# Moving transposes of exponentials behind the transposes of x, and two row sums into the following stage, in a fused attention and MLP kernel

## The chip, the cores and the metric

One core of a Trainium2 chip. The metric is the device time of one execution in microseconds; the median of three runs of the kernel before is 269.20 us (269.05 to 269.24).

The names of the engines are those of the profile: PE multiplies matrices (PEld is its loading of weights), DVE is the vector engine, ACT the scalar engine, POOL the general one, and SP issues transfers. Each has its own program and they meet at semaphores.

## The reference

Linear attention (a softmax of q over the head's 64 columns, one of k over the 576 positions) over 8 batches with 8 heads, followed by a layer norm and an MLP with a residual:

```python
q_s = exp(q - max(q, -1));  q_s = q_s / sum(q_s, -1)
k_s = exp(k - max(k, 2));   k_s = k_s / sum(k_s, 2)
kv  = einsum('bhsd,bhse->bhde', k_s, v)
x   = einsum('bhsd,bhde->bhse', q_s, kv)       # then to (8, 576, 512)
xn  = (x - mean(x)) / sqrt(var(x) + 1e-6) * g_ln
out = x + relu(xn @ w_ch1) @ w_ch2             # 512 -> 2048 -> 512
```

## The kernel before

**Chunks and stages.** The positions of each batch are cut into 512 main ones (4 tiles of 128) and 64 remaining ones. The 8 batches' main parts are chunks 0 to 7; the remaining 8 x 64 rows together are a ninth, `C9`, the last chunk. The kernel has one stage for each chunk: PE does the two MLP multiplications of chunk c, while the attention of chunk c+1 and the first steps of c+2 are worked in between. I call "stage c" the stage that multiplies chunk c.

**An order written out by hand.** In each stage `mlp_steps(c)` gives a list of PE steps with a weight each, and a list `side` gives (position, function) pairs for all other work. `run` walks through the PE steps, adds up the weights, and emits a side function as soon as the sum has reached its position. The order in which they are emitted is the order of the instructions on each engine: each engine's program is fixed, and nothing is sorted anew later. A position is thus a place in a queue, not a time.

**The two multiplications.** From stage 2 on both are done with seven products in place of eight (a Strassen form). The first, `mm1_fast`, takes positions 0 to 56: two halves, each with two groups (0 and 1, then 2 and 3) of seven products of four matmuls, in the order 1, 5, 6, 2, 7, 3, 4; each product is done for both groups of the half, and a matmul of 256 columns weighs 0.5. So product 5 takes positions 4 to 8, product 6 takes 8 to 12, product 7 takes 16 to 20, product 4 takes 24 to 28. All products go to banks of PSUM, six in rotation (`mm_ps`), by names x, b, c. Products 1, 6, 7 and 4 of a group accumulate into its bank x. Between them, DVE reads the bank: `add_5` (L775) after product 6, `out_22` (L778) after product 7. Each is emitted right after the last matmul of its group, and the group's next product into that bank waits for it:

```python
plan = (
    (1, "x", True, seed), (5, "b", True, copy_5), (6, "x", False, add_5),
    (2, "c", False, lambda g: out_relu(g, "c", 0, 0)), (7, "x", False, out_22),
    (3, "b", False, lambda g: out_relu(g, "b", 0, 1)),
    (4, "x", False, lambda g: out_relu(g, "x", 1, 0)),
)
```

The second, `mm2_fast`, takes positions 56 to 112, 8 for each product in the order 1, 5, 6, 2, 7, 3, 4. At its end DVE scales the results, adds x and writes the output tiles (`y_quarter`, L610, from the banks named c, e, b, a), after two additions (`add_u`, L627). The next stage's product 5 takes the banks that these steps free.

**Side work of a stage c.** For chunk c+1 (`attn_fast`): the reciprocal of the row sums of exp(q) (`recip_q`, L859); `kv_all`, 40 small matmuls and on DVE L342 and L344; per tile t the attention product `po_mm` and, on DVE, `x_fast` (L421 and L407, which write x and the scaled xn). Two transfers transpose xn, `xn_T`, two tiles each, from SP's queue; then `sum_x` (L248) forms four differences of the transposed x, which products 5, 6, 7 and 4 of the next stage take. They run on POOL, for chunk 7 the second on DVE, for the last chunk all on DVE. For chunk c+2 (`prep_fast`): exp(q) on ACT (`exp_q`), its transpose by a transfer of SP (`eq_T`, L256), its row sums on DVE in two halves (`reduce_q`, L210, 128x1024 to 128x16), exp(k) (`exp_k`). SP's queue also holds the loads of the next batch (`load_batch`), emitted at position 1, and in stage 6 those of the last chunk (`load_qrem`).

Batch 3 and the last chunk are apart: batch 3's exponentials, transpose and first sum stand in `second_side` (stage 1) and its second sum at position 8 of stage 2; the last chunk's exponentials, transpose and both sums stand in stage 6 (at the end of the file), and what follows of it in `attn_rest` (stage 7).

Of the kernel before, what the change touches and what calls it, by code (L numbers as in the profile page):

```python
# [20 lines left out]
def kernel(  # L21
# [31 lines left out]
    C9 = B  # L53
# [795 lines left out]

    def prep_fast(b):  # L850

        s = [(57, lambda: exp_q(b, 0, 4)), (65, lambda: exp_q(b, 2, 4)), (70, lambda: eq_T(b))]
        s += [(81, lambda: reduce_q(b, 0, 2)), (91, lambda: reduce_q(b, 2, 2))]
        s += [(81, lambda: exp_k(b, 0, 4)), (98, lambda: exp_k(b, 2, 4))]
        s += [(106, lambda: prep_kvrem(b))]
        return s

    def recip_q(c):
        nc.vector.reciprocal(eqs[c][2], eqs[c][1])  # L859

    def attn_fast(c):

        s = [(8, lambda: reduce_q(3, 2, 2))] if c == 3 else []
        s += [(22 if c == 3 else 2, lambda: recip_q(c))]
        s += [(12, lambda: kv_all(c))]
        s += [(40, lambda: start_x(c))]
        for t, (p0, p1) in enumerate(((48, 53), (57, 59), (65, 67), (73, 75))):
            s += spread([lambda t=t, i=i: po_mm(c, t, i) for i in range(NP)], p0, p1)
            s += [(p1, lambda t=t: x_fast(c, t)), ((66, 74, 87, 91)[t], lambda t=t: square_sum(c, t))]
        s += [(61, lambda: xn_T(c, 0, 2)), (78, lambda: xn_T(c, 2, 2)), (95, lambda: rstd_op(c))]  # L870
        s += [((84, 100 if c == C9 - 1 else 88, 92, 101)[i], lambda i=i: sum_x(c, i)) for i in range(4)]
        return s

    def second_side():

        s = [(p, lambda i=i: quarter_w2(i, 1)) for i, p in enumerate((8.5, 13, 44, 46))]
        s += [(8.0, lambda: xn_pT(1, 3, nc.vector))]
        s += [(3, lambda: exp_q(2, 0, 4)), (7, lambda: exp_q(2, 2, 4)), (7.2, lambda: eq_T(2))]
        s += [(42, lambda: square_sum(1, 2)), (67, lambda: square_sum(1, 3)), (71, lambda: rstd_op(1))]
        s += [(7.3, lambda: load_batch(3, (2,), eqTs[2][0:1, T - 1, NP - 1, 0:4])), (31, lambda: load_batch(3, (0,)))]  # L880
        s += [(9 + 2 * j, lambda j=j: cast_v(2, j)) for j in range(2)]
        s += [(7.4, lambda: load_v(3))]
        s += [(93 + j, lambda j=j: cast_v(3, j)) for j in range(2)]
        s += [(15 + 3 * t, lambda t=t: reduce_q(2, t, 2)) for t in (0, 2)]
        s += [(36, lambda: recip_q(2))]
        s += [(18, lambda: exp_k(2, 0, 4)), (22, lambda: exp_k(2, 2, 4)), (26, lambda: prep_kvrem(2))]
        s += [(41, lambda: kv_all(2))]
        s += [(46, lambda: start_x(2))]
        for t, (p0, p1) in enumerate(((52, 54), (57, 59), (62, 65), (70, 74))):
            s += spread([lambda t=t, i=i: po_mm(2, t, i) for i in range(NP)], p0, p1)  # L890
            s += [(p1, lambda t=t: x_fast(2, t)), ((73, 82, 88, 94)[t], lambda t=t: square_sum(2, t))]
        s += [(60, lambda: xn_T(2, 0, 2)), (77, lambda: xn_T(2, 2, 2)), (100, lambda: rstd_op(2))]
        s += [(75, lambda: exp_q(3, 0, 4)), (79, lambda: exp_q(3, 2, 4)), (85, lambda: eq_T(3))]
        s += [(97, lambda: reduce_q(3, 0, 2))]
        s += [(97, lambda: exp_k(3, 0, 4)), (108, lambda: exp_k(3, 2, 4)), (113, lambda: prep_kvrem(3))]
        s += [(p, lambda i=i: sum_w1(i, 1)) for i, p in enumerate((30, 47, 58, 64))]
        s += spread([lambda i=i: sum_x(2, i) for i in range(4)], 95, 108)
        return s

    def attn_rest():  # L900

        s = [(2, lambda: recip_q(C9)), (4, lambda: start_x(C9))]
        for t, (p0, p1, p2) in enumerate(((14, 22, 46), (44, 54, 62), (58, 66, 69), (67, 75, 77))):
            s += [(p0, lambda t=t: [po_mm(C9, t, i) for i in range(NP)])]
            s += [(p1, lambda t=t: x_fast(C9, t)), (p2, lambda t=t: square_sum(C9, t))]
        s += [(61, lambda: xn_T(C9, 0, 2)), (78, lambda: xn_T(C9, 2, 2)), (88, lambda: rstd_op(C9))]
        return s + spread([lambda i=i: sum_x(C9, i) for i in range(4)], 102, 104)
# [179 lines left out]
    with tc.manual_schedule(  # L1087
        engines={mybir.EngineType.PE, mybir.EngineType.DVE, mybir.EngineType.Activation,
                 mybir.EngineType.SP, mybir.EngineType.Pool}
    ):  # L1090
        first_batch()
        load_behind(1, (2, 0))
        load_w2(2)
        load_behind(1, (1,))
        load_w2(3)
        load_behind(2)

        def po_x(c, t):
            for i in range(NP):
                po_mm(c, t, i)  # L1100
            x_fast(c, t)

        run(
            mlp_steps(0),
            [
                (0.5, lambda: xn_pT(0, 1, nc.scalar)),
                (2.5, lambda: (q0_rest(2), x_fast(0, 2))),
                (3.2, lambda: eq_pT(0, 3, nc.scalar)),
                (7, lambda: (q0_rest(3), x_fast(0, 3))),
                (11, lambda: xn_pT(0, 2, nc.scalar)),  # L1110
                (15, lambda: xn_pT(0, 3, nc.scalar)),
                (20, g_columns),
                (24, lambda: square_sum(0, 2)),
                (28, lambda: square_sum(0, 3)),
                (34, lambda: (x_copy(0, 0), square_po(0, 1))),
                (36, lambda: x_copy(0, 1)),
                (37, lambda: nc.vector.tensor_scalar_mul(out=xs[0][3][:, 0, 1:2], in0=xs[0][3][:, 0, 1:2], scalar1=float(DM))),
                (38, lambda: rstd_op(0)),
            ]
            + [(62, lambda: exp_q(1, 0, 4)), (64, lambda: exp_q(1, 2, 4))]  # L1120
            + [(67 + t, lambda t=t: reduce_q(1, t)) for t in range(T)]
            + [((74, 78, 86, 90)[t], lambda t=t: eq_pT(1, t, nc.scalar)) for t in range(T)]
            + [(78, lambda: nc.vector.reciprocal(eqs[1][2], eqs[1][1]))]
            + [(80, lambda: exp_k(1, 0, 4)), (84, lambda: exp_k(1, 2, 4))]
            + [(26 + 4 * i, lambda i=i: scale_w1(i % KO1, i // KO1)) for i in range(2 * KO1)]
            + [(p, lambda i=i: quarter_w2(i, 0)) for i, p in enumerate((55, 58, 60, 62))]
            + [(98.5 + 0.4 * j, lambda j=j: cast_v(1, j)) for j in range(2)]
            + [(p, lambda i=i: sum_w1(i, 0)) for i, p in enumerate((80, 84, 88, 92))]
            + [(100.4, lambda: prep_kvrem(1))]
            + [(100.5, lambda: kv_mm(1, range(T))), (102.0, lambda: (kv_mm(1, range(T, T + 1)), kv_out(1), start_x(1)))]  # L1130
            + [(108.0, lambda: po_x(1, 0)), (110.0, lambda: po_x(1, 1))]
            + [(113.0, lambda: po_x(1, 2)), (114.9, lambda: xn_pT(1, 0, nc.scalar)), (115.9, lambda: square_sum(1, 0))]
            + [(115.9, lambda: po_x(1, 3)), (121.0, lambda: xn_pT(1, 1, nc.scalar)), (122.0, lambda: square_sum(1, 1))]
            + [(128.0, lambda: xn_pT(1, 2, nc.scalar))]

        )
        for c in range(1, B):
            side = []
            if c == 1:
                side += second_side()  # L1140
            else:
                if c + 1 < B:
                    side += attn_fast(c + 1)
                else:
                    side += attn_rest()
                if c + 2 < B:
                    side += [(1, lambda b=c + 2: load_batch(b))]
                    side += [(26, lambda b=c + 2: load_v(b))]
                    side += prep_fast(c + 2)
            if c == B - 2:  # L1150
                side += [(1, load_qrem)]
                side += spread([lambda r=r: exp_qrem(r) for r in range(T)], 58, 80)
                side += [(84, lambda: eq_T(C9))]
                side += [(84 + 4 * t, lambda t=t: reduce_q(C9, t, 2)) for t in (0, 2)]
            sums = [(57, 0)] if c == FAST else [(p, i) for i, p in enumerate((30, 41) if c == B - 1 else (30, 33, 41))]
            run(mlp_steps(c), side + [(at, lambda i=i: sum_h(0, i)) for at, i in sums])
        run(mlp_steps(C9), [(33 + 3 * i, lambda i=i: sum_h(0, i)) for i in range(2)])
# [30 lines left out]
```

## Time and profile before

| what | value |
|---|---|
| median of 3 runs | 269.20 us |
| the profiled execution | 269.13 us |
| its span, first to last instruction | 267.3 us |
| granted clock of PE, mean | 0.993 |
| PE busy | 259.4 us, 97% |
| DVE busy | 219.9 us, 82% |
| ACT busy | 178.9 us, 67% |
| POOL busy | 90.8 us, 34% |
| row sums `reduce_q` on DVE | 20 of 1.05 us mean, 20.6 us |
| transposes of exp(q) issued by SP | 7, landing after 4.9 us (median) |
| transposes of xn issued by SP | 14, landing after 3.5 us (median) |

The profile gives for each instruction its engine, the line of the kernel, the tiles that it writes and reads (out<-in) and its start and duration. In the timeline, neighbours of one line and form are merged (x2, x8), with the idle time of the engine before them and what ended it in brackets. On DVE an instruction starts up to 0.09 us before the one ahead of it is reported as ended, so costs in a full queue are spacings from start to start rather than durations. A matmul of 256 columns is listed with 0.27 us, but the next one starts 0.109 us after it.

### The profile page before, as it was taken

What the parts mean: (1) busy time and instruction counts of PE and PEld (TensorE: products, weight loads), DVE (VectorE), ACT (ScalarE), POOL (GpSimd) and SP (SyncE); (2) the same over time, 40 slices, a digit from 0 to 9 for tenths busy, and PEclk for the clock granted to TensorE, in tenths of its full rate; (3) what the DMA queues carried; (4) which work ended last, traced back from release to release, by engine and by line L of the source; (5) the groups of instructions that cost most, each with busy time, mean ns of one, the idle gap of its engine ahead of it and who ended that gap; (6) DMA issues with size and microseconds to landing.
All of it is one profiled execution on the core that took longest, in us unless ns stands there. A gap on an engine that the chain in (4) does not pass through costs nothing. (4 is left out here: it accounts for less than half of the span.)

```text
span 267.3 us, 6695 instructions
## 1 busy us (share of the span) xinstructions
PE 259.4 (97%) x2631; PEld 219.1 (82%) x2634; DVE 219.9 (82%) x471; ACT 178.9 (67%) x349; POOL 90.8 (34%) x145
## 2 busy tenths in 40 slices
PE   8899999999999999999999999999999899999993
PEld 6688855675888998899889988998898788888882
DVE  7864885887999899789978997898799968877872
ACT  4667881697966886688668866886678378438400
POOL 6943126213059203940394059206400800030000
PEclk9899999999999999999999999999999999999999
DMA  6999999978975996799699939995805430422014
GB/s 209 222 201 207 323 225 297 268 189 263 180 142 161 324 163 94 240 288 97 117 264 265 142 71 274 267 154 108 256 2 97 100 122 4 78 81 78 2 39 118
DMA packets 82329, 45.00 MB, mean 168 GB/s; under 512 B 58037, under 2 KB 78521, under 8 KB 82298
## 3 DMA queue, kind: packets, MB, share of 16 engines
q0 software_dynamic: 32800, 22.29, 46.1%
q1 hardware_dynamic: 48906, 21.77, 36.5%
q10 hardware_dynamic: 592, 0.52, 0.6%
q8 instruction: 20, 0.33, 0.5%
q14 instruction: 11, 0.09, 0.1%
HBM read 36.70 MB, written 9.44 MB: 173 GB/s over the span
## 5 line engine op out<-in xcount | busy, mean ns | idle before, releaser
L599 PEld LDWEIGHTS <-hs 128*128 128x128 bf16 x512 | 49.5, 98 | 5.7
L744 PEld LDWEIGHTS <-w_q 128*128 128x128 bf16 x448 | 42.9, 98 | 6.7 <-DVE ot L610 1.0
L248 POOL TENSOR_TENSOR tq<-xnT 128x256 bf16<-128x256 bf16 x24 | 15.6, 665 | 78.1 <-DMA xnT<-xn 40.2
L599 PEld LDWEIGHTS <-hT 128*128 128x128 bf16 x384 | 37.2, 98 | 4.4
L744 PEld LDWEIGHTS <-w1g 128*128 128x128 bf16 x336 | 32.2, 98 | 3.9
L599 PE MATMUL ba<-w_q,hs 128*128 128x256 bf16 x256 | 31.7, 273 | 0.0
L775 DVE TENSOR_TENSOR bb<-bx,s 128x512 f32<-128x512 f32 x28 | 18.2, 695 | 13.9 <-ACT s L772 13.9
L744 PE MATMUL bx<-tq,w_q 128*128 128x256 bf16 x224 | 29.0, 273 | 0.0
L768 ACT COPY bc<-bx 128x512 f32<-128x512 f32 x28 | 15.2, 596 | 16.8 <-PE bx L744 16.8
L421 DVE SCALAR_TENSOR_TENSOR x<-po,rq 128x512 bf16<-128x512 f32 x34 | 23.3, 686 | 2.4 <-PE po L370 2.1
L395 ACT ACTIVATE scrap<-x,mv 128x512 bf16<-128x512 bf16 x32 | 23.0, 719 | 1.6 <-DVE x L421 1.3
L616 POOL DMA_DIRECT2D out_dram<-ot x28 | 15.4, 557 | 24.1 <-DVE ot L610 24.0
L786 ACT ACTIVATE hT<-bc 128x512 bf16<-128x512 f32 x28 | 15.3, 595 | 12.1 <-PE bc L744 12.1
L583 DVE TENSOR_TENSOR hs<-hT 128x1024 bf16<-128x1024 bf16 x32 | 21.7, 686 | 1.3 <-ACT hT L786 1.2
L210 DVE TENSOR_REDUCE zq<-eq 128x16 f32<-128x1024 bf16 (+1 forms) x20 | 20.6, 1047 | 0.9 <-ACT eq L193 0.8
L370 PE MATMUL po<-kv_sb,eqT 128*128 128x128 bf16 x128 | 21.1, 219 | 0.0
L786 ACT ACTIVATE hT<-bb 128x512 bf16<-128x512 f32 x28 | 15.2, 595 | 8.8 <-PE bb L744 8.8
L778 DVE TENSOR_TENSOR hT<-bx,s 128x512 bf16<-128x512 f32 x28 | 18.0, 685 | 3.2 <-PE bx L744 3.2
L624 ACT COPY s<-ba 128x512 f32<-128x512 f32 x15 | 8.7, 578 | 12.5 <-PE ba L599 7.8
L599 PE MATMUL ba<-w_sb,hT 128*128 128x256 bf16 x128 | 16.7, 273 | 0.0
L599 PE MATMUL bb<-w_q,hs 128*128 128x256 bf16 x128 | 16.6, 273 | 0.0
L772 ACT COPY s<-bb 128x512 f32<-128x512 f32 x28 | 15.7, 624 | 1.0 <-PE bb L744 0.9
(152 smaller groups left out, 555.3 us busy)
## 6 DMA issues: line engine op xcount, KB each, us to landing
out_dram<-ot POOLq DMA_DIRECT2D x32, 256.0 KB, 6.1
qt<-in_q_dram SPq DMA_DIRECT2D x5, 1024.0 KB, 5.9
kt<-in_k_dram SPq DMA_DIRECT2D x5, 1024.0 KB, 12.8
w_sb<-in_moe_w_ch_dram POOLq DMA_DIRECT2D x4, 512.0 KB, 17.2
qt<-in_q_dram POOLq DMA_DIRECT2D x2, 1024.0 KB, 15.0
kt<-in_k_dram POOLq DMA_DIRECT2D x2, 1024.0 KB, 15.7
vm<-in_v_dram POOLq DMA_DIRECT2D x16, 128.0 KB, 11.2
w_raw<-in_moe_w_ch_dram POOLq DMA_DIRECT2D x3, 512.0 KB, 12.6
```

Of the source, the lines that this page charges most:

```text
L210: nc.vector.reduce_sum(eqs[c][1][:, ts], eqs[c][0][:, ts], axis=AX.X)
L248: eng.tensor_tensor(out=dst[:, t], in0=x[:, t], in1=y[:, t], op=ALU.subtract)
L370: nc.tensor.matmul(pobox["p"][:, i * P : i * P + P], eqTs[c][:, t, i, :], kv_sb[:, c, i, :], start=True, stop=True,)
L395: nc.scalar.activation(scrap, x[:, t], AF.Square, bias=mv[:, t, 0:1], scale=-float(DM), accum_out=mv[:, t, 1:2],)
L421: nc.vector.scalar_tensor_tensor(x[:, t].rearrange("p (h d) -> p h d", h=H), in0=pobox[c, t].rearrange("p (h d) -> p h d", h=H), scalar=1. ...
L583: nc.vector.tensor_tensor(out=dst, in0=x, in1=y, op=op)
L599: nc.tensor.matmul(hbox[bank][:, t], lhsT, rhs, start=first and (own or t == 0) and k == 0, stop=k == KH - 1, skip_group_check=True)
L744: nc.tensor.matmul(dst[:, q], lhsT, rhs, start=first and q == 0 and ko == 0, stop=ko == 1, skip_group_check=True)
L772: nc.scalar.copy(at[g, "s"], at[g, "b"])
L775: nc.vector.tensor_tensor(out=at[g, "b"], in0=at[g, "x"], in1=at[g, "s"], op=ALU.add)
L778: nc.vector.tensor_tensor(out=h_out(g, 1, 1), in0=at[g, "x"], in1=at[g, "s"], op=ALU.add)
L786: nc.scalar.activation(h_out(g, odd, half), at[g, name], AF.Relu)
```

## The change

Three sorts of moves; no operation is added or removed.

1. The transpose of exp(q) of batches 4 to 7 (`prep_fast`, stages 2 to 5) goes from position 70 to 79. The second transpose of xn is at 78, the first at 61, so the three now follow one another as xn, xn, exp(q) on SP.
2. Batch 3's first row sum leaves the end of stage 1 (position 97) for position 10 of stage 2, the second goes there from 8 to 18, the reciprocal from 22 to 26.
3. The last chunk's second row sum leaves the end of stage 6 (position 92) for position 6 of stage 7, where the reciprocal goes from 2 to 12; its transpose and first sum go from 84 to 88 in stage 6.

```diff
 def prep_fast(b):
-        s = [(57, lambda: exp_q(b, 0, 4)), (65, lambda: exp_q(b, 2, 4)), (70, lambda: eq_T(b))]
+        s = [(57, lambda: exp_q(b, 0, 4)), (65, lambda: exp_q(b, 2, 4)), (79, lambda: eq_T(b))]
...
 def attn_fast(c):
-        s = [(8, lambda: reduce_q(3, 2, 2))] if c == 3 else []
-        s += [(22 if c == 3 else 2, lambda: recip_q(c))]
+        s = [(p, lambda t=t: reduce_q(3, t, 2)) for t, p in ((0, 10), (2, 18))] if c == 3 else []
+        s += [(26 if c == 3 else 2, lambda: recip_q(c))]
...
 def second_side():
-        s += [(97, lambda: reduce_q(3, 0, 2))]
...
 def attn_rest():
-        s = [(2, lambda: recip_q(C9)), (4, lambda: start_x(C9))]
+        s = [(6, lambda: reduce_q(C9, 2, 2)), (12, lambda: recip_q(C9)), (4, lambda: start_x(C9))]
...
             if c == B - 2:
-                side += [(84, lambda: eq_T(C9))]
-                side += [(84 + 4 * t, lambda t=t: reduce_q(C9, t, 2)) for t in (0, 2)]
+                side += [(88, lambda: eq_T(C9))]
+                side += [(88, lambda: reduce_q(C9, 0, 2))]
```

## The prediction, before the changed kernel had run

> **What bounds the kernel now.** I began with the page: how much of the span PE (TensorE) is busy. Then a stretch of one stage.
>
> ```profile
> span 267.3 us, 6695 instructions
> PE 259.4 (97%) x2631; PEld 219.1 (82%) x2634; DVE 219.9 (82%) x471; ACT 178.9 (67%) x349; POOL 90.8 (34%) x145
> ```
>
> ```profile
> 122.20:148.40 26.20, 26.20 (x283) 23.42 (x281) 22.82 (x49) 19.61 (x39) 12.05 (x18) 1.00 1.05 186
> ```
>
> In the second row the columns after the stretch are its length and the busy time of PE, PEld, DVE, ACT, POOL. PE is busy for all of 26.20 us, so the stages of batches 3 to 6 cannot get shorter by removing waits. The first products of the stages of batches 2 to 7 and of the last chunk start at 79.50, 106.06, 132.27, 158.48, 184.69, 210.90 and 238.36 us: the stages of 3 to 6 take 26.21 each, that of 2 takes 26.56 and that of 7 27.46. What PE still waits for there is in its list of waits (total, times, longest):
>
> ```profile
> PE bb L744 <- DVE ot L610: 0.9, 2, 0.7
> PE bb L744 <- DVE kt L1079: 0.2, 1, 0.2
> ```
>
> Matmuls of 256 columns start 0.109 us apart. Counted from start to start, the first row is two holes in stage 7: 212.63 instead of 211.77 (0.86) and 213.41 instead of 213.07 (0.34). The second is one hole in stage 2: 81.16 instead of 80.82 (0.34; I use 0.33). All three are bank "b" of product 5 waiting until DVE has read the last stage's results out of that bank (L610).
>
> **The vector engine at these places.** The timeline (start, duration) across the start of stage 2:
>
> ```profile
> 76.16 1.21 DVE L210 TENSOR_REDUCE zq<-eq 128x16 f32<-128x1024 bf16 x1
> ...
> 81.04 1.21 DVE L210 TENSOR_REDUCE zq<-eq 128x16 f32<-128x1024 bf16 x1
> ...
> 82.29 1.30 DVE L775 TENSOR_TENSOR bb<-bx,s 128x512 f32<-128x512 f32 x2
> ```
>
> The first sum (76.16) stands ahead of the six result steps L610; the second behind them, in the slot before the addition L775, which waits for product 6 anyway. And in stage 6, which has no sums there:
>
> ```profile
> 187.13 1.30 DVE L775 TENSOR_TENSOR bb<-bx,s 128x512 f32<-128x512 f32 x2 [1.10 <-ACT s L772]
> ...
> 188.34 0.17 DVE L342 RECIPROCAL rzk<-pkv 128x4 f32<-128x4 f32 x1
> 188.54 0.86 DVE L344 TENSOR_TENSOR kv_sb<-pkv,rzk 64x256 bf16<-64x256 f32 x2
> ...
> 189.69 1.29 DVE L778 TENSOR_TENSOR hT<-bx,s 128x512 bf16<-128x512 f32 x2 [0.28 <-PE bx L744]
> ...
> 190.80 1.04 PE L744 MATMUL bx<-tq,w1g 128*128 128x256 bf16 x8
> ```
>
> The 8 matmuls at 190.80 are product 4 of groups 0 and 1; each overwrites the bank "x" that output step L778 of its group reads. L778 of group 1 starts 190.29 and ends 190.98; product 4 of group 1 starts at 190.80 + 4 x 0.109 = 191.24. So there is 0.26 us of slack in that place, and a sum takes 1.2.
>
> **The change, part by part.**
>
> *Batch 3's sums.* The first leaves the end of stage 1. Its neighbours there run without gaps, so it holds them for 76.16 to 77.29, 1.13 us. Once gone, the last L610 pair waits for the end of product 4 instead, as at the start of stage 6, where PE has no hole: gain 0.33, all of it.
>
> Both sums then stand at positions 10 and 18 of stage 2. Four matmuls weigh 2, so in program order position 10 falls between L775 of group 0 and of group 1, and 18 between L778 of group 0 and of group 1. The slot ahead of L775, where one was free, stays empty. I put them into stage 6's rows: L775 of group 0 at 187.13; +0.61 to the next start; +1.13 sum; +0.60 L775 of group 1; +0.20 L342; +0.78 the two L344; +0.61 L778 of group 0; +1.13 sum; +0.69 L778 of group 1 until its end: 192.88. With 0.05 to PE's start (212.58 to 212.63 at the hole) product 4 of group 1 starts at 192.93 instead of 191.24: 1.69, say 1.7. On the way product 7 of group 1 waits some 0.1 and product 4 of group 0 some 0.3; these are part of the 1.7, since PE starts its products in order. Later DVE has 1.04 us free before the next L775 (89.29), so nothing more is late; the reciprocal L859 is needed only by L421 some 4 us on (197.60 in stage 6). Stage 2 takes 26.21 + 1.7 = 27.9 instead of 26.56.
>
> The bounds: least is the second sum alone, with L778 of group 0 on time: (0.61 + 1.13 + 0.69) from 189.69 gives 192.12, +0.05, hence 0.93. Most is full durations in place of spacings, 0.08 more at seven steps: 2.25. I take 1.7, since each step's spacing comes from the same form.
>
> That DVE lets no later step pass is the premise. The rows show starts in program order only. The Trainium skill, Perfetto Trace Analysis, "Tensor Engine Instruction (MATMUL, LD_WEIGHTS)", says the same of DVE: a strict queue, and only PE may take weight loads early; were that wrong the sum would be that of the first rival.
>
> *The last chunk's second sum* leaves the end of stage 6:
>
> ```profile
> 207.63 1.20 DVE L210 TENSOR_REDUCE zq<-eq 128x16 f32<-128x1024 bf16 x1
> 208.29 2.64 POOL L248 TENSOR_TENSOR tq<-xnT 128x256 bf16<-128x256 bf16 x4 [17.93 <-DMA xnT<-xn]
> 208.99 1.42 DVE L248 TENSOR_TENSOR tq<-xnT,tq 128x256 bf16<-128x256 bf16 x2 [0.15 <-POOL tq L248]
> ...
> 212.50 0.86 DVE L610 SCALAR_TENSOR_TENSOR ot<-ba,rstd,x 128x256 f32<-128x256 f32 x2
> ...
> 213.28 0.34 DVE L859 RECIPROCAL rq<-zq 128x32 f32<-128x32 f32 x1
> ...
> 214.54 0.70 DVE L775 TENSOR_TENSOR bb<-bx,s 128x512 f32<-128x512 f32 x1 [0.92 <-ACT s L772]
> ```
>
> The sum at 207.63 delays nothing: DVE's next step, L248, begins only once POOL's first difference is there (208.95), and that starts at 208.29 because the transposed x has just landed. Behind it DVE runs without a gap to the last L610. Without the sum, DVE idles from 207.71 to 208.99 and the holes of 0.86 and 0.34 stay. The gain is 0; at most, if the differences came earlier too, 1.13.
>
> In stage 7 the sum takes the place of the reciprocal: 213.28 + 1.21 = 214.49, just before 214.54, where L775 waits for product 6. The reciprocal moves into the 0.84 us that DVE idles before 216.68. Cost 0; if that cover is missed by a little, L775 is 0.1 late, and product 7 behind it has more room than that (216.21 against 215.84).
>
> *The last chunk's transpose and first sum, 84 to 88:* on SP it stays behind the two transposes of x, on DVE behind L627 and before L610. No instruction changes places: 0.
>
> *Transposes of batches 4 to 7, 70 to 79,* in stages 2 to 5. Stage 5's SP queue, as issues:
>
> ```profile
> 177.02 2.72 SPq L256 DMA_TRANSPOSE eqT<-eq  x1
> 179.87 1.23 SPq L256 DMA_TRANSPOSE xnT<-xn  x1
> ```
>
> The second transpose of x is ready at 177.79 and now goes first; in stage 6, where it already does, it took 4.10 us from issue to landing (204.03 to 208.13), so POOL's differences can start at about 181.9 instead of 183.13. PE has no hole for them to fill: gain 0. The other transpose is issued until about 182 instead of 179.74. Only SP's loads stand behind it, and the next, at 183.02, waited for L179 on ACT; the transposed tile is read from position 48 of the next stage, over 10 us on. Cost 0.
>
> Sum: -0.33 + 1.7 + 0 + 0 = +1.4. The profiled execution took 269.13 us (span 267.35), so 270.5 there; the median shown, 269.20, is 0.07 above it: **270.6 us**.
>
> **The rivals.**
> - *The sums cost nothing in stage 2* (not slower). Place: L778 of group 1. If DVE is through with it by 86.0 (191.24 in stage 2's time), PE never waits and only the gain of 0.33 less some 0.1 at product 7 is left: 269.0. For it: DVE idles 1.10 and 0.28 us there. Against it: these gaps lie before L775 and L778 of group 0, ahead of the sums in program order. Chance 7%.
> - *The holes of stage 7 close too,* with stage 2's loss: 270.6 - 1.1 = 269.5. For it: DVE has no gap from 208.99 on. Against it: the step at 208.99 waits for POOL. Chance 6%. Together with the first rival it would be 267.9; 5%.
> - *POOL's earlier differences collide with DVE.* L248 on DVE takes 0.75 us beside POOL's L248 and 0.285 alone. If they met the two L583 in stages 2 to 5, that is 2 x 0.46 less 0.2 of slack (the last L610 ends at 185.77, product 5 of group 1 starts at 186.00), 0.7 each: 270.6 + 4 x 0.7 = 273.4. Against: the L583 end at 178.99, 2.9 us before POOL can start. The Trainium skill, SBUF — State Buffer, "Who interferes with whom", has DVE steps with two SBUF inputs and GpSimd's reads block each other; by that rule the trace's 0.75 is explained. Chance 4%.
>
> **How the numbers follow.** The forecast has 78%, with its own range 269.8 (stall 0.93) to 271.2 (2.25 with the hole closed). The range of 8 in 10 adds the case of 269.5: 269.4 to 271.2. A change under 0.2% (0.54 us) can't be told from none: within are the first rival and the closed holes, 13%; faster is the pair of them, 5%; slower is the forecast and the collision, 82%.
>
> **What would show it.** Right: after, PE has no hole before product 5 in stage 2, and new waits of product 4 on L778 of 1 to 1.7 us; stage 2 takes 27.9; stage 7's two holes are still there, with DVE idle about 1.2 us before L248; POOL's differences begin about 1 us earlier in stages 2 to 5, whose length is else 26.2. Wrong: a stage 2 of 26.2, or stage 7's holes gone.

## The result and the profile after

The changed kernel takes 270.46 us (median of 7 runs, 269.93 to 270.85) against 269.24 of the kernel before (median of 7, 268.89 to 269.86): a ratio of 1.0037, with a 95% interval of 1.0021 to 1.0052. It is slower by 1.2 us. One of the twelve runs of an experiment below (the first sum left, the second later) took 542.15 us, twice as long as the others, and no ratio counts it.

The span of the profiled execution grew from 267.35 to 269.07 us. Where this went is read from the stretches of whole stages, first product to first product of the next: stage 2, stage 3 and stage 7. The columns after the stretch are its length and the busy time of PE, PEld, DVE, ACT and POOL, then PE's granted clock and the share and GB/s of the transfers. Before:

```profile
79.50:106.06 26.56, 26.39 (x283) 23.34 (x280) 24.56 (x52) 19.72 (x38) 10.43 (x17) 1.00 1.07 187
106.06:132.27 26.21, 26.21 (x283) 23.44 (x280) 22.93 (x49) 19.62 (x38) 11.47 (x18) 1.00 1.03 189
210.90:238.36 27.46, 26.60 (x259) 22.50 (x257) 22.53 (x54) 15.69 (x33) 3.88 (x8) 1.00 0.21 59
```

After:

```profile
79.81:107.81 28.00, 26.66 (x282) 23.36 (x280) 24.92 (x51) 19.84 (x38) 12.37 (x20) 1.00 0.97 177
107.81:134.02 26.21, 26.21 (x282) 23.43 (x280) 22.83 (x49) 19.62 (x38) 11.90 (x19) 1.00 1.03 189
212.65:240.10 27.45, 26.59 (x258) 22.52 (x256) 23.64 (x55) 15.69 (x33) 3.88 (x8) 1.00 0.21 59
```

Only stage 2 has another length: 28.00 instead of 26.56 us, 1.44 more. Stages 3 to 6 take 26.21 as before, stage 7 takes 27.45. The other 0.3 us of the span lies ahead of stage 2 (its first product starts at 79.81 instead of 79.50). There the two kernels differ only by the sum that left DVE's queue at the end of stage 1, and PE starts that late or later in kernels that keep this sum too (80.07 in the first experiment below): it is scatter, as the last section shows. In stage 7 DVE is 1.1 us busier, with the sum that came to it, and PE is not.

PE's list of waits after the change (total, times, longest):

```profile
PE bx L744 <- DVE hT L778: 1.3, 2, 1.1
...
PE bb L744 <- DVE ot L610: 0.9, 2, 0.7
```

The row "PE bb L744 <- DVE kt L1079" (stage 2's hole at product 5) is gone, and in its place stands a wait for L778, which the list of before does not have. The row of stage 7 is unchanged. The timeline of stage 2 before the change, DVE and PE, with the hole at product 5 (81.16) and none at product 7 (84.21) or 4 (85.95):

```profile
80.38 0.61 PE L744 MATMUL bb<-tq,w_q 128*128 128x256 bf16 x4
...
81.16 0.60 PE L744 MATMUL bb<-tq,w_q 128*128 128x256 bf16 x4 [0.17 <-DVE kt L1079]
...
84.21 1.04 PE L744 MATMUL bx<-tq,w_q 128*128 128x256 bf16 x8
84.84 1.29 DVE L778 TENSOR_TENSOR hT<-bx,s 128x512 bf16<-128x512 f32 x2 [0.28 <-PE bx L744]
...
85.95 1.04 PE L744 MATMUL bx<-tq,w1g 128*128 128x256 bf16 x8
```

And after it:

```profile
80.68 1.04 PE L744 MATMUL bb<-tq,w_q 128*128 128x256 bf16 x8
...
82.25 0.70 DVE L775 TENSOR_TENSOR bb<-bx,s 128x512 f32<-128x512 f32 x1 [1.36 <-ACT s L772]
...
82.86 1.21 DVE L210 TENSOR_REDUCE zq<-eq 128x16 f32<-128x1024 bf16 x1
...
83.98 0.69 DVE L775 TENSOR_TENSOR bb<-bx,s 128x512 f32<-128x512 f32 x1
84.17 1.16 PE L744 MATMUL bx<-tq,w_q 128*128 128x256 bf16 x8
...
84.79 0.86 DVE L344 TENSOR_TENSOR kv_sb<-pkv,rzk 64x256 bf16<-64x256 f32 x2
85.16 1.04 PE L744 MATMUL bb<-xnT,w_q 128*128 128x256 bf16 x8
85.68 0.69 DVE L778 TENSOR_TENSOR hT<-bx,s 128x512 bf16<-128x512 f32 x1
86.28 1.21 DVE L210 TENSOR_REDUCE zq<-eq 128x16 f32<-128x1024 bf16 x1
...
86.43 0.61 PE L744 MATMUL bx<-tq,w1g 128*128 128x256 bf16 x4 [0.23 <-DVE hT L778]
87.41 0.68 DVE L778 TENSOR_TENSOR hT<-bx,s 128x512 bf16<-128x512 f32 x1
...
88.15 0.60 PE L744 MATMUL bx<-tq,w1g 128*128 128x256 bf16 x4 [1.11 <-DVE hT L778]
```

DVE idles 1.36 us ahead of the first L775, in the slot where a sum stood before: the sum that stands behind L775 did not go ahead of it. DVE then works through two sums with the additions and outputs pinned behind them. Product 4 of group 0 (86.43) starts when the first L778 is through, that of group 1 (88.15) when the second is. From start to start, PE's holes in this stage are 0.12 (product 7 of group 1, inside the row at 84.17, which lasts 1.16 us and not 1.04), 0.39 and 1.27 us: 1.78 together.

The timeline at the start of stage 7 after the change, where the last chunk's second sum was taken out ahead of it, POOL, DVE and PE:

```profile
210.04 2.64 POOL L248 TENSOR_TENSOR tq<-xnT 128x256 bf16<-128x256 bf16 x4 [19.84 <-DMA xnT<-xn]
210.74 1.42 DVE L248 TENSOR_TENSOR tq<-xnT,tq 128x256 bf16<-128x256 bf16 x2 [1.27 <-POOL tq L248]
...
214.38 0.61 PE L744 MATMUL bb<-tq,w_q 128*128 128x256 bf16 x4 [0.69 <-DVE ot L610]
215.03 1.20 DVE L210 TENSOR_REDUCE zq<-eq 128x16 f32<-128x1024 bf16 x1
215.16 0.60 PE L744 MATMUL bb<-tq,w_q 128*128 128x256 bf16 x4 [0.17 <-DVE ot L610]
...
216.29 1.30 DVE L775 TENSOR_TENSOR bb<-bx,s 128x512 f32<-128x512 f32 x2
```

Ahead of L248, DVE now waits 1.27 us for POOL where it waited 0.15, and both holes (0.86 and 0.33) stay. The sum in its new place ends at 216.23, some 0.05 us ahead of the addition at 216.29. Last, the timeline of SP's issues in stage 5 after the change:

```profile
177.28 3.52 SPq L256 DMA_TRANSPOSE xnT<-xn  x2
180.94 2.04 SPq L256 DMA_TRANSPOSE eqT<-eq  x1
```

The three transposes stand in the new order. POOL's differences now start 3.46 us ahead of stage 6's first product (182.98 against 186.44) instead of 1.56 (183.13 against 184.69), and the stage is as long as before.

### The profile page after: what moved, and what is told of

Same layout as the page of the kernel before. It is cut to its first block, busy times and chain, and to the rows that moved or that the text cites. A ratio compares the mean times of both kernels' runs of the same rounds, so it can differ in the third digit from the quotient of the medians.

```text
span 269.1 us, 6698 instructions
## 1 busy us (share of the span) xinstructions
PE 260.3 (97%) x2634; PEld 219.9 (82%) x2634; DVE 220.1 (82%) x471; ACT 178.8 (66%) x349; POOL 90.6 (34%) x145
## 5 line engine op out<-in xcount | busy, mean ns | idle before, releaser
L744 PEld LDWEIGHTS <-w_q 128*128 128x128 bf16 x448 | 43.0, 98 | 6.4 <-DVE ot L610 1.0
L248 POOL TENSOR_TENSOR tq<-xnT 128x256 bf16<-128x256 bf16 x24 | 15.6, 665 | 78.4 <-DMA xnT<-xn 53.3
L744 PEld LDWEIGHTS <-w1g 128*128 128x128 bf16 x336 | 32.1, 98 | 5.7 <-issue 1.3
L775 DVE TENSOR_TENSOR bb<-bx,s 128x512 f32<-128x512 f32 x28 | 18.3, 694 | 14.3 <-ACT s L772 13.3
L744 PE MATMUL bx<-tq,w_q 128*128 128x256 bf16 x224 | 29.2, 273 | 0.0
L583 DVE TENSOR_TENSOR hs<-hT 128x1024 bf16<-128x1024 bf16 x32 | 21.6, 683 | 1.3 <-ACT hT L786 1.2
L778 DVE TENSOR_TENSOR hT<-bx,s 128x512 bf16<-128x512 f32 x28 | 18.1, 684 | 2.7 <-PE bx L744 2.7
L786 ACT ACTIVATE hT<-bx 128x512 bf16<-128x512 f32 x28 | 15.4, 604 | 1.3 <-PE bx L744 1.3
## 6 DMA issues: line engine op xcount, KB each, us to landing
kt<-in_k_dram SPq DMA_DIRECT2D x5, 1024.0 KB, 13.5
```

The source lines that it names most:

```text
L248: eng.tensor_tensor(out=dst[:, t], in0=x[:, t], in1=y[:, t], op=ALU.subtract)
L583: nc.vector.tensor_tensor(out=dst, in0=x, in1=y, op=op)
L744: nc.tensor.matmul(dst[:, q], lhsT, rhs, start=first and q == 0 and ko == 0, stop=ko == 1, skip_group_check=True)
L775: nc.vector.tensor_tensor(out=at[g, "b"], in0=at[g, "x"], in1=at[g, "s"], op=ALU.add)
L778: nc.vector.tensor_tensor(out=h_out(g, 1, 1), in0=at[g, "x"], in1=at[g, "s"], op=ALU.add)
L786: nc.scalar.activation(h_out(g, odd, half), at[g, name], AF.Relu)
```

## The experiments

Each was run beside the kernel before on one chip; the ratio is to that kernel. "Undone" and "only" refer to the three sorts of moves of the change.

**Batch 3's sums undone, all else kept.**

```diff
-        s = [(p, lambda t=t: reduce_q(3, t, 2)) for t, p in ((0, 10), (2, 18))] if c == 3 else []
-        s += [(26 if c == 3 else 2, lambda: recip_q(c))]
+        s = [(8, lambda: reduce_q(3, 2, 2))] if c == 3 else []
+        s += [(22 if c == 3 else 2, lambda: recip_q(c))]
...
+        s += [(97, lambda: reduce_q(3, 0, 2))]
```

> The changed kernel with batch 3's two sums and reciprocal back where they were (97 in stage 1, 8 and 22 in stage 2); the moved transposes and the last chunk's moved sum stay. My theory: the whole loss is made by batch 3's sums and the other moves are worth nothing, so 269.2 us (-0.2 to +0.2 of the kernel before), stage 2 takes 26.56 us with its hole of 0.34 at product 5, stage 7 keeps its holes of 0.86 and 0.34, and product 4 waits for nothing. Rival (the other moves cost or gain a part of the 1.2): 268.5 or 269.8 and a stage other than 2 with another length than before.

Measured: 269.23 us, ratio 0.9996 (0.9979 to 1.0013). Stage 2 takes 26.55 us, with its hole of 0.33 at product 5; stages 3 to 6 take 26.21 and stage 7 27.45, with holes of 0.86 and 0.33. The moved transposes and the last chunk's moved sum together are worth nothing, stage by stage.

**Batch 3's sums only,** in the kernel before: the same edit the other way.

> The kernel before with only batch 3's sums and reciprocal moved (10, 18, 26 of stage 2). My theory: all of the loss, 270.5 us, stage 2 takes 28.0 us with product 4 held 1.2 to 1.7 us by L778, the other stages as before. Rival (the loss needs the moved transposes too, as their transfers or POOL's earlier differences disturb stage 2): between 269.2 and 270, with stage 2 below 27.5.

Measured: 270.62 us, ratio 1.0058 (1.0037 to 1.0079). Stage 2 takes 28.00 us; its holes are 0.13, 0.39 and 1.27, the same as in the changed kernel. All of the loss is made by this part alone, without the new order of the transposes.

**The first sum ahead of L775, the second left between the two L778.**

```diff
-        s = [(p, lambda t=t: reduce_q(3, t, 2)) for t, p in ((0, 10), (2, 18))] if c == 3 else []
+        s = [(p, lambda t=t: reduce_q(3, t, 2)) for t, p in ((0, 8), (2, 18))] if c == 3 else []
```

> The changed kernel with batch 3's first sum at 8 (ahead of L775 of group 0) and the second left at 18 (between L778 of group 0 and of group 1). My theory: only the second sum costs, 0.61 + 1.13 + 0.69 + 0.05 us from the start of L778 of group 0 against PE's demand 1.55 us after it: one hole of about 0.9 before product 4 of group 1 and none elsewhere; stage 2 takes 27.1 us, 269.8 us in all. Rival (the second sum's whole 1.2 us or nothing goes to PE): stage 2 of 27.4 or more, or of 26.3.

Measured: 269.78 us, ratio 1.0015 (1.0002 to 1.0027); stage 2 takes 27.13 us. Its timeline:

```profile
84.56 0.69 DVE L778 TENSOR_TENSOR hT<-bx,s 128x512 bf16<-128x512 f32 x1 [0.28 <-PE bx L744]
...
85.17 1.21 DVE L210 TENSOR_REDUCE zq<-eq 128x16 f32<-128x1024 bf16 x1
...
86.29 0.68 DVE L778 TENSOR_TENSOR hT<-bx,s 128x512 bf16<-128x512 f32 x1
...
87.03 0.60 PE L744 MATMUL bx<-tq,w1g 128*128 128x256 bf16 x4 [0.76 <-DVE hT L778]
```

DVE is on time here: it idles 0.28 us before the first L778, as in the kernel before. One sum between the two outputs then makes one hole, 0.92 us from start to start, and no other.

**The first sum left between the two L775, the second later,** at 36, ahead of the L775 of the second half; the reciprocal at 50.

```diff
-        s = [(p, lambda t=t: reduce_q(3, t, 2)) for t, p in ((0, 10), (2, 18))] if c == 3 else []
-        s += [(26 if c == 3 else 2, lambda: recip_q(c))]
+        s = [(p, lambda t=t: reduce_q(3, t, 2)) for t, p in ((0, 10), (2, 36))] if c == 3 else []
+        s += [(50 if c == 3 else 2, lambda: recip_q(c))]
```

> The changed kernel with batch 3's first sum left at 10 (between the two L775) and the second at 36, the reciprocal at 50. My theory: the first sum makes everything of DVE behind it late by 1.13, of which the slack takes a part: holes of 0.12 at product 7 of group 1, about 0.4 at product 4 of group 0 and about 0.1 at that of group 1; stage 2 takes 26.8 to 26.9, 269.6 us in all. Rival (the first sum is covered, only the second costs): stage 2 of 26.2 to 26.3, 268.9 us.

Measured: 269.70 us, ratio 1.0009 (0.9993 to 1.0026). Stage 2 takes 27.07 us, not 26.8 to 26.9: the holes of 0.13, 0.40 and 0.14 in the first half came as expected, and a fourth of 0.16, which I had not expected, at product 7 in the second half, which waits for L775 behind the second sum. The first sum alone costs 0.67 us of PE in the first half, against 0.92 of the second one alone, though no wait of it is long; it is not covered. (Why DVE was late in the second half is told in the last section.)

**Both sums ahead of an L775:** positions 8 and 36, the reciprocal at 50.

```diff
-        s = [(p, lambda t=t: reduce_q(3, t, 2)) for t, p in ((0, 10), (2, 18))] if c == 3 else []
-        s += [(26 if c == 3 else 2, lambda: recip_q(c))]
+        s = [(p, lambda t=t: reduce_q(3, t, 2)) for t, p in ((0, 8), (2, 36))] if c == 3 else []
+        s += [(50 if c == 3 else 2, lambda: recip_q(c))]
```

> The changed kernel with batch 3's sums at positions 8 and 36 of stage 2 (each ahead of an L775 that DVE reaches 1.0 to 1.4 us too early) and the reciprocal at 50. My theory: it is the place between the two L775 and the two L778 that costs, not that the sums are in stage 2. The hole of 0.34 at product 5 goes and none comes: 268.9 us, stage 2 takes 26.2 to 26.4. Rival (stage 2 has no room on DVE for two sums, wherever they stand): a stage 2 of 27 or more, 269.6 us or above.

Measured: 268.95 us, ratio 0.9983 (0.9967 to 1.0000), and stage 2 takes 26.21 us, without a hole. Its timeline, DVE alone:

```profile
80.69 1.21 DVE L210 TENSOR_REDUCE zq<-eq 128x16 f32<-128x1024 bf16 x1
...
82.12 1.30 DVE L775 TENSOR_TENSOR bb<-bx,s 128x512 f32<-128x512 f32 x2 [0.22 <-ACT s L772]
...
84.67 1.29 DVE L778 TENSOR_TENSOR hT<-bx,s 128x512 bf16<-128x512 f32 x2 [0.28 <-PE bx L744]
...
88.12 1.21 DVE L210 TENSOR_REDUCE zq<-eq 128x16 f32<-128x1024 bf16 x1
89.25 1.28 DVE L775 TENSOR_TENSOR bb<-bx,s 128x512 f32<-128x512 f32 x2
```

The two sums are the same work in the same stage. In the slots ahead of L775, where DVE waits anyway, they cost nothing, and the move then keeps its gain at the end of stage 1. The time of 0.24 us below the kernel before is at the edge of its interval; the stage's length is the stronger evidence.

**Chunk 7's second difference on POOL,** in the kernel before, with both of the last chunk's sums left where they were.

```diff
-        eng = nc.vector if c == C9 or (c == C9 - 1 and i == 1) else nc.gpsimd
+        eng = nc.vector if c == C9 else nc.gpsimd
...
-        s += [((84, 100 if c == C9 - 1 else 88, 92, 101)[i], lambda i=i: sum_x(c, i)) for i in range(4)]
+        s += [((84, 88, 92, 101)[i], lambda i=i: sum_x(c, i)) for i in range(4)]
```

> The kernel before with one thing changed: chunk 7's second difference of the transposed x (L248, position 100 of stage 6) runs on POOL at position 88, as it does for chunks 3 to 6, and not on DVE. Both of the last chunk's sums stay at the end of stage 6. My theory: stage 7's holes of 0.86 and 0.34 come from DVE's wait for POOL's first difference and the 1.35 us of L248 behind it, so both go: 268.0 us, stage 7 takes 26.2 to 26.3. Rival (the sums at the end of stage 6 make DVE late): the holes stay within 0.3 us of what they were, 269.0 or above.

Measured: 267.76 us, ratio 0.9947 (0.9930 to 0.9964). Stage 7 takes 26.26 us instead of 27.45, and its holes are gone. The timeline of the turn from stage 6 to 7, with POOL, DVE and PE:

```profile
207.83 1.21 DVE L210 TENSOR_REDUCE zq<-eq 128x16 f32<-128x1024 bf16 x1
208.49 1.29 POOL L248 TENSOR_TENSOR tq<-xnT 128x256 bf16<-128x256 bf16 x2 [18.15 <-DMA xnT<-xn]
208.96 0.69 DVE L627 TENSOR_TENSOR bb<-bb,s 128x512 f32<-128x512 f32 x1
...
211.10 1.04 PE L744 MATMUL bx<-xnT,w1g 128*128 128x256 bf16 x8
211.30 0.88 DVE L610 SCALAR_TENSOR_TENSOR ot<-ba,rstd,x 128x256 f32<-128x256 f32 x2
211.97 1.04 PE L744 MATMUL bb<-tq,w_q 128*128 128x256 bf16 x8
```

The second sum still stands at 207.83, and L627 follows it at once. What had held DVE was the difference in its queue, and not the sum. This run takes away two things at once, the difference's wait for POOL and its own time on DVE (from 208.99 to the L627 at 210.33 in the kernel before, 1.34 us), and does not tell them apart; in the changed kernel, with the sum gone and the difference left, the wait took the sum's place.

**Both together:** positions 8 and 36, and the difference on POOL, in the changed kernel.

> The changed kernel with batch 3's sums at 8 and 36 (reciprocal at 50) and chunk 7's second difference on POOL at 88. My theory: both gains add, since they are holes of PE in two stages: 269.2 - 0.34 - 1.2 = 267.7 us, stages 2 to 7 all between 26.2 and 26.4 us. Rival (one gain is given back in the last chunk's stage, which needs POOL's stores or differences earlier): 268.2 or above with a longer stage 7 or last stage.

Measured: 267.54 us, ratio 0.9932 (0.9917 to 0.9948). Stage 2 takes 26.29 us (one hole of about 0.08 is left, in product 7 of the second half), stages 3 to 6 take 26.21 and stage 7 26.26. The gains add up, and this version is faster than both kernels, by 1.7 us or 0.7% against the one before. That it beats the difference on POOL alone (267.76, run beside other runs of the kernel before) is not shown by the medians; the lengths of stage 2, 26.29 and 26.56, say that it does, by some 0.3 us.

## Why the prediction was right

- *Gain at the end of stage 1, 0.33:* right. The hole at product 5 of stage 2 is gone; the last pair L610 waits for product 4 (80.01 us, 0.20 after stage 2's first product), as at the start of stage 6.
- *Loss in stage 2, 1.69:* right in mechanism and size; the three holes sum to 1.78 us where 0.1, 0.3 and the rest of 1.7 were forecast. The 0.09 is mostly one spacing: from the first L344 (84.79) to L778 (85.68) DVE took 0.89 us where I had put 0.78. 0.78 is the row's 0.86 less 0.08, as if the step behind an L344 started early like others; in the trace it starts 0.01 to 0.03 us after the L344 has ended. The premise that DVE lets no later step pass is borne out by its 1.36 us of idling ahead of L775 with a sum behind it. The bounds of 0.93 and 2.25 held too, and the lower one is a kernel now: with the second sum between the L778 and the first ahead of both L775, the hole is 0.92.
- *Stage 2 of 27.9 us:* measured 28.00. The other stages moved by no more than 0.01.
- *Last chunk's second sum, 0:* right, with DVE idle 1.27 us (forecast about 1.2) and the holes of 0.86 and 0.33 unmoved; the sum's new place was hit with 0.05 us to spare. That the difference in DVE's queue makes these holes, and not the sum, was argued in the prediction and is shown by the run with the difference on POOL; which part of it the wait for POOL makes in the kernel before is not shown.
- *Transposes, 0:* right in effect. One size was off: in stage 5 POOL's differences start 1.9 us earlier against the next stage (1.5 to 2.5 us in stages 2 to 5), not about 1 us, because the transpose of x landed 3.25 us after its issue (179.57 to 182.82) and not 4.10 as in stage 6. No cost of the earlier start shows: the stages are of the same length.
- *The sum, 1.4:* the difference of the medians is 1.22 us, that of the stages 1.44 - 0.01. The interval of the ratio is 0.57 to 1.40 us, so the stages' 1.43 lies just above its upper end; batch 3's sums alone, in the second experiment, cost 1.43 between medians too. (The upper end of the prediction's range, 271.2, comes out of its own terms as 271.1: 269.20 + 2.25 - 0.33.)
- *The rivals:* that the sums cost nothing where they were put fell with the waits on L778; that stage 7's holes close by the sum's leaving fell with the 1.27 us of idle DVE; a collision of the earlier differences with DVE's L583 did not show.

In all, the change did for stage 1 what its place in the queue allows, gained nothing where PE had no hole to fill (the transposes) or where another wait ended last (stage 7), and lost in stage 2 because two of the sums were put between steps that the next product waits for.

## What to carry to other kernels

In a queue that runs in a fixed order, what a moved step costs is decided by the step directly behind it and by how soon another engine needs that one: the same two sums in the same stage cost 1.78 us of PE time between the steps of a pair and nothing ahead of a pair, where the engine waits anyway. Before a step is moved to relieve a full queue, look at what ends the queue's last wait ahead of the trouble; here an engine that seemed to have no gap was held by one difference that waits for another engine, and taking work out ahead of it only lengthened the wait. A stage's length from first product to first product shows such effects of a few tenths of a microsecond far more sharply than the time of the run.

## What I had not expected of the hardware

The scatter between executions lies almost wholly ahead of stage 2. Over the nine profiled executions here, one of each kernel, stage 2's first product starts between 78.46 and 80.07 us, a range of 1.6 us, while stages 3 to 6 take 26.21 us each in all nine and the holes that several of them share come back within 0.06 us. A median that moves by 0.3 us between two versions says little; the stages say it.

Part of this scatter goes with PE's granted clock. In eight of the nine profiles the clock is at half for one stretch of 3.4 us that begins 10.8 to 13.5 us into the span; in the ninth (the first sum left, the second later) there is no such stretch, and its stage 2 starts at 78.46 us, 1.0 us ahead of any other (79.50 to 80.07). The mean clock of the timed runs separates them too: with both sums ahead of an L775, the five runs at 0.999 or 1.000 took 267.82 to 268.55 us, the seven at 0.994 or less 268.83 to 269.30. What makes the clock drop in most runs and not in all, no run here shows.

One step of DVE, the in-place maximum L783 in stage 2, takes 0.43 us in six of the nine profiles, and 0.68, 0.67 and 0.77 us in the three with the second sum at 36 (both sums ahead of an L775; the first left at 10; both ahead and the difference on POOL). The traces tell with what this goes: POOL is issuing the loads of v at that time (L147, mostly 0.91 to 0.94 us each). Of the 126 steps L783 in the nine profiles 27 take more than 0.45 us. Of these, 22 start 0.22 to 0.70 us after the start of such an issue and end 1.16 to 1.19 us after it; the other five stand in the same way to a shorter issue, L150, and end 0.84 to 0.86 us after its start. No L783 that starts 0.22 to 0.70 us after an L147 takes only 0.43 us, and apart from the five none that starts outside these bounds takes more. In stage 2 L783 starts 0.41 to 0.51 us after an issue in the three kernels, and 0.77 us or more after one in the other six. What follows L783 is not the reason: L583, which reads what it wrote, follows it directly in these three kernels and the reciprocal in the other six, but in stage 6 of the kernel before L583 follows it too (191.01), and it takes 0.43 us.

This is also where the two small holes of the second half come from. With the difference on POOL as well, L783 took 0.08 us more than with both sums ahead alone (0.77 instead of 0.68), every step of DVE from there to L775 followed in the same spacing, and product 7 waited the 0.08. With the first sum left at 10, L783 took 0.24 us more than 0.43; without them, by the same spacings, L775 would have been through before PE asked for it, and the hole of 0.16 would not be there. That is worked out from the rows; no run moved POOL's issues.
